# First feed-forward's weights loaded a second time, two bytes off, so that one mask gives the low half's 25 bits

## Chip, cores and metric

One core of one Trainium2 chip. The metric is device microseconds for one execution of the whole program, the median of three runs.

## What is computed

Eight images of 576 tokens go through a packed attention (32 packed queries, 8 heads of 64), then through two feed-forwards. The first is the one that the change touches:

```python
h = x @ w_in                                   # x 4608x512, w_in 512x2048
g = h * (1.0 / (1.0 + np.exp(-1.702 * h)))
x = (g @ w_out).astype(np.float32)             # w_out 2048x512
h = np.maximum(np.maximum(x @ w1, x @ w2), x @ w3)
out = (h @ w_out2).astype(np.float32)
```

`w_in` and `w_out` arrive as float64, eight bytes a number. The kernel sees each number as two 32-bit words, low word first.

## The kernel before

**Numbers in two parts.** TensorE multiplies fp32r operands. To keep float32 accuracy every operand is held as a high and a low part, and `mm3` (lines 102 to 104) makes a product of three matmuls: low by high, high by low, high by high.

**Conversion of a weight.** `load_raw` (L136) brings one raw tile of 128 x 2048 words on the SP queue as two DMAs of 512 KB. `convert` (L142) makes from it, on 1024 numbers per partition, the high part (rounded down to what fp32r holds) and the low part (the bits of the double that come below). In the text a step of it goes by its line:

- L148, DVE: the high word without sign and without its lowest 9 bits, into `tmp`; L149, ACT: its exponent put on float32's scale.
- L151, DVE: the lowest 9 bits of the high word, into the second half of `tmp`.
- L152, DVE: the 16 bits under them, read as a uint16 view of the low word, times 2^-16, added to L151's result. So the low part has 25 bits, built from two places of the raw double.
- L154, DVE: sign and L149's result joined; L157, ACT: the high part written to the weight tile.
- L158, DVE: sign and exponent alone, written back over the high word; L159, DVE: L152's 25 bits times 2^-20 times that power of two, the low part of the weight tile.

So a conversion has six DVE instructions and two ACT instructions, each over 128 x 1024. There are sixteen: for each quarter `n` of the hidden width two of `w_in` (`wi0_n`, `wi1_n`) and two of `w_out` (`wo4n`, `wo4n+2`).

**Tiles.** Raw tiles, `tmp`, finished weights and `pw` (the attention's packed values multiplied into `w_in`, one tile for each image and quarter) share one pool, `w_tile`, of 16 buffers of 8 KB per partition. The eight `wo` tiles stay for the whole feed-forward. A new tile waits for the last reader of the one that had its buffer.

**Stages.** Attention of images 0 and 1 comes first, the conversions run beside it and beside the first units of the feed-forward. A unit `n` is one (image, half of the tokens, 128 hidden columns): `h_unit` makes `h` on TensorE, takes tanh on ACT (L495) and joins it on DVE (`t`, L496); `g_unit` splits the result (ACT L501, DVE L503); `out_unit`, two units later, adds it to four `acc` banks. At the end of four or eight units DVE and ACT move `acc` out (L523, L527, L529). The units of images 0 and 1 go by quarters of the hidden width, so each quarter of the weights is first read at a certain unit: quarter 1 at unit 16, quarter 2 at unit 32, quarter 3 at unit 36. Images 0 and 1 take 64 units, and from the 64th on nothing is converted for this feed-forward. The second feed-forward ends the program.

**What sets the order.** Every step is put in a list with a time of its own (`add`), the list is sorted and traced, and the tile framework's scheduler then orders each engine's instructions and places the tiles. At run time each engine, and the SP queue, goes through its instructions strictly in that order.

Of the kernel before, what the change touches and what calls it, by code (L numbers as in the profile page):

```python
# [10 lines left out]
I32 = mybir.dt.int32  # L11
U16 = mybir.dt.uint16
AF = mybir.ActivationFunctionType
ALU = mybir.AluOpType
# [6 lines left out]
TB = 512  # L21
# [12 lines left out]
L_ = [8.18, 16.49, 4, 22.39]  # L34
Z_ = [1, 1, 1, 0, 0, 0, 0, 0, 0, 0, 0, 0, 0, 0, 0, 0]
# [7 lines left out]
def tile_packed_attention_moe(  # L43
# [13 lines left out]
    nc = tc.nc  # L57
# [19 lines left out]
    def f(t):  # L77
        return t.bitcast(F32)

    def i(t):  # L80
        return t.bitcast(I32)


    def w_tile(name, dt=F32R):
        return wp.tile([P, 2, 2, TB], dt, tag="w", name=name)
# [29 lines left out]
    rebias = const.tile([P, 1], F32, name="rebias")  # L115
# [20 lines left out]
    def load_raw(name, srcs):  # L136
        raw = w_tile(f"raw_{name}", I32)
        for x, src in enumerate(srcs):
            nc.sync.dma_start(raw[:, x].rearrange("p a b -> p (a b)"), src)
        return raw  # L140

    def convert(name, raw, pool):  # L142
        h = raw.rearrange("p x a (b w) -> p (x a b) w", w=2)[:, :, 1]
        m = raw.bitcast(U16).rearrange("p x a (b w) -> p (x a b) w", w=4)[:, :, 1]
        tmp = w_tile(f"tmp_{name}", I32)
        t1, t2 = (tmp[:, x].rearrange("p a b -> p (a b)") for x in range(2))
        w = w_tile(name)
        nc.vector.tensor_scalar(out=t1, in0=h, scalar1=0x7FFFFE00, scalar2=None, op0=ALU.bitwise_and)  # L148
        nc.scalar.activation(t1, t1, AF.Relu, scale=8.0, bias=rebias)  # L149
        yield  # L150
        nc.vector.tensor_scalar(out=t2, in0=h, scalar1=0x1FF, scalar2=None, op0=ALU.bitwise_and)  # L151
        nc.vector.scalar_tensor_tensor(out=f(t2), in0=m, scalar=2.0 ** -16, in1=t2, op0=ALU.mult, op1=ALU.add)  # L152
        yield
        nc.vector.scalar_tensor_tensor(  # L154
            out=t1, in0=h, scalar=-2 ** 31, in1=t1, op0=ALU.bitwise_and, op1=ALU.bitwise_or
        )
        nc.scalar.copy(w[:, :, 0], f(tmp[:, 0]))  # L157
        nc.vector.tensor_scalar(out=h, in0=t1, scalar1=-2 ** 23, scalar2=None, op0=ALU.bitwise_and)  # L158
        nc.vector.scalar_tensor_tensor(  # L159
            out=w[:, :, 1], in0=f(tmp[:, 1]), scalar=2.0 ** -20,  # L160
            in1=f(raw).rearrange("p x a (b w) -> p x (a b) w", w=2)[:, :, :, 1], op0=ALU.mult, op1=ALU.mult
        )
        yield w
# [246 lines left out]
    wi = {}  # L410
# [39 lines left out]
    wo = {}  # L450
# [94 lines left out]
    def c_tile(name):  # L545
        if "f" in late:
            return late["r"].tile([P, TB], F32R, tag="c", name=name)
        return u_tile(name, F32R)[:, :TB]

    def conv_late(name, raw, hi, lo, n):  # L550
        t1, t2 = (late["r"].tile([P, TB], I32, tag="c", name=f"c{y}_{name}") for y in range(2))
        h = raw.rearrange("p (a w) -> p a w", w=2)[:, :, 1]
        m = raw.bitcast(U16).rearrange("p (a w) -> p a w", w=4)[:, :, 1]
        nc.vector.tensor_scalar(out=t1, in0=h, scalar1=0x7FFFFE00, scalar2=None, op0=ALU.bitwise_and)
        nc.scalar.activation(t1, t1, AF.Relu, scale=8.0, bias=rebias)
        nc.vector.tensor_scalar(out=t2, in0=h, scalar1=0x1FF, scalar2=None, op0=ALU.bitwise_and)
        nc.vector.scalar_tensor_tensor(out=f(t2), in0=m, scalar=2.0 ** -16, in1=t2, op0=ALU.mult, op1=ALU.add)
        nc.vector.scalar_tensor_tensor(
            out=t1, in0=h, scalar=-2 ** 31, in1=t1, op0=ALU.bitwise_and, op1=ALU.bitwise_or
        )  # L560
        nc.scalar.copy(hi, f(t1))
        nc.vector.tensor_scalar(out=h, in0=t1, scalar1=-2 ** 23, scalar2=None, op0=ALU.bitwise_and)
        nc.vector.scalar_tensor_tensor(
            out=lo, in0=f(t2), scalar=2.0 ** -20, in1=f(raw).rearrange("p (a w) -> p a w", w=2)[:, :, 1],
            op0=ALU.mult, op1=ALU.mult
        )
        return f(t1), f(t2)


    class Piece:  # L570
# [11 lines left out]
        def conv(self):  # L582
            self.hl = [c_tile(f"wa{y}_{self.n}") for y in range(2)]
            self.v, self.s = conv_late(self.n, self.raw, *self.hl, TB)
# [213 lines left out]
    def add(t, fn, *a):  # L798
        plan.append((t, len(plan), fn, a))

    def conv(t, name, src, store, load=6.0, pool=0, step=0.0):
        raws, it = [], []

        def a():
            raws.append(load_raw(name, src))

        def b_():
            it.append(convert(name, raws[0], pool))
            next(it[0])

        def c_():
            next(it[0])

        def d_():
            store(next(it[0]))

        add(t - load, a)
        add(t, b_)
        add(t + step, c_)
        add(t + 2 * step, d_)  # L820
# [13 lines left out]
    def main():  # L834
# [10 lines left out]
        t = T0  # L845
# [13 lines left out]
        def wi_save(g, n):  # L859
            nc.gpsimd.dma_start(f(wsc[g, n].rearrange("c p a b -> p c a b")), f(sv[g, n]))  # L860

        def wi_store(g, n):
            def s(ws):
                sv[g, n] = ws
                if W_[n] == 0:
                    wi_save(g, n)
                for c in range(2):
                    wi[0, 2 * g + c, n] = ws[:, c]
            return s

        def wo_store(fc):
            def s(ws):
                wo[fc], wo[fc + 1] = (ws[:, x] for x in range(2))
            return s

        kk = 0
        for n in range(NQ):
            def tc_(kk):
                base = 7 + 6.49 * kk if n == 0 else tn[start[0, n]] - 22 + 7 * (kk - 4 * n)
                return base + K_[kk]  # L880
            for g in range(2):
                t = tc_(kk)
                conv(t, f"wi{g}_{n}", [w_in[2 * g, n], w_in[2 * g + 1, n]], wi_store(g, n), L_[kk] if kk < 4 else 19, Z_[kk], 0.0)
                if W_[n] > 0:
                    add(t + W_[n], wi_save, g, n)
                kk += 1
                for b in range(2):
                    add(max(t + .1, tn[start[b, n]] - PL_[b], tpt[b, g]), pw1_unit, b, g, n)
            for fc in range(4 * n, 4 * n + 4, 2):
                conv(tc_(kk), f"wo{fc}", [w_out[fc], w_out[fc + 1]], wo_store(fc), L_[kk] if kk < 4 else 19, Z_[kk], 0.0)  # L890
                kk += 1


# [35 lines left out]
        for idx in range(18):  # L929
            pc = Piece(idx // 2, idx % 2)  # L930
            t = TP + idx * TP_[1] if idx < 14 else TB0 - 10 + (idx - 14) * 10.5
# [5 lines left out]
        for fc in range(NF2):  # L937
            t = max(TP + 14 * TP_[1] + TP_[2] * fc, tn[225])
# [39 lines left out]
    if True:  # L978
        main()
        for _, _, fn, a in sorted(plan, key=lambda s: s[:2]):  # L980
            fn(*a)
        late["f"].release()
        late["x"].release()
        spp.release()
# [53 lines left out]
```

## Time and profile before

| | |
|---|---|
| median of 3 runs | 1418.73 us (1418.44 to 1420.18) |
| the profiled execution's own time | 1418.77 us |
| its span, first to last instruction | 1416.9 us |
| busy: TensorE (PE) | 1344.9 us, 95% of the span |
| busy: VectorE (DVE) | 989.1 us, 70% |
| busy: ScalarE (ACT) | 575.2 us, 41% |
| busy: GpSimd (POOL) | 322.6 us, 23% |
| read from HBM / written | 191.89 MB / 43.78 MB |

Busy time is the union of an engine's instructions. A matmul's end is modelled, so PE's share says where PE was held up rather than how near it is to its peak. [...]

### The profile page before, as it was taken

The page shows a single profiled execution, that of the slowest core. Times are in us where ns is not written, and L with a number is a line of the kernel's source. Part 1 is how long each engine was busy: PE and PEld are TensorE (multiplying, and loading weights), DVE is VectorE, ACT ScalarE, POOL GpSimd, SP SyncE. Part 2 cuts the span into 40 slices and gives each one's busy share as a digit, 9 for nine tenths or more (in the row PEclk, how much of TensorE's full clock was granted, in tenths as well). Part 3 has the DMA queues.
Part 4 walks back from the last instruction along what each step waited for, and adds up shares of the span by engine and source line. Part 5 has one row for each costly group of instructions (what it writes and reads, how often), then busy time and mean ns, then how long its engine had stood idle before and what let it go on. Part 6 is the DMA issues. An engine that isn't in the chain of part 4 may idle for free.

```text
span 1416.9 us, 22472 instructions
## 1 busy us (share of the span) xinstructions
PE 1344.9 (95%) x8450; PEld 1278.2 (90%) x8450; DVE 989.1 (70%) x1850; ACT 575.2 (41%) x1212; POOL 322.6 (23%) x436
## 2 busy tenths in 40 slices
PE   5899789999999999999999899699999999999998
PEld 3688789999999989999888899699989999899997
DVE  6799897887666566759899977564646646466362
ACT  3555555664554555545555552131221311213111
POOL 1110244344331035314344222101101001011000
PEclk8999899999999999999999999899999999999999
DMA  8654313561442224125655539765747747476461
GB/s 310 240 189 150 113 55 108 160 198 42 124 127 77 94 66 131 58 75 190 201 173 173 172 126 299 256 227 174 258 161 248 269 160 250 169 259 216 144 205 45
DMA packets 88524, 237.13 MB, mean 167 GB/s; under 512 B 10848, under 2 KB 40032, under 8 KB 81504
## 3 DMA queue, kind: packets, MB, share of 16 engines
q0 software_dynamic: 24640, 132.66, 27.8%
q1 hardware_dynamic: 63776, 103.05, 21.9%
q8 instruction: 66, 1.08, 0.3%
q14 instruction: 42, 0.34, 0.1%
HBM read 191.89 MB, written 43.78 MB: 166 GB/s over the span
## 4 chain that ended last, share of the span: by engine, by line
PE 75%; DVE 16%; DMA 3%; issue 2%; ACT 2%; POOL 1%; SPq 1%; DVEq 0%; ACTq 0%; POOLq 0%
PE p L102 9%; PE p L103 8%; PE p L104 8%; PE acc L102 7%; PE acc L103 7%; PE acc L104 7%; PE accb L103 3%; PE accb L104 3%; PE accb L102 3%; PE h L102 3%; PE h L104 3%; PE h L103 3%; DVE g L503 2%; DVE t L496 2%; DMA xr<-x2d 1%
## 5 line engine op out<-in xcount | busy, mean ns | idle before, releaser
L102 PE MATMUL acc<-g,wo 128*128 128x288 f32 x1024 | 306.3, 302 | 16.2 <-DVE x L523 5.9
L103 PE MATMUL acc<-g,wo 128*128 128x288 f32 x1024 | 303.8, 297 | 7.6 <-DVE g L503 7.5
L104 PE MATMUL acc<-g,wo 128*128 128x288 f32 x1024 | 303.7, 297 | 0.0
L102 PEld LDWEIGHTS acc<-g,wo 128*128 128x128 f32 x1024 | 194.4, 191 | 22.6 <-issue 6.3
L103 PEld LDWEIGHTS acc<-g,wo 128*128 128x128 f32 x1024 | 195.2, 191 | 12.6 <-DVE g L503 10.2
L104 PEld LDWEIGHTS acc<-g,wo 128*128 128x128 f32 x1024 | 195.2, 191 | 0.7 <-issue 0.3
L503 DVE TENSOR_TENSOR g<-t,g 128x288 fp32r<-128x288 f32 x254 | 142.6, 562 | 44.4 <-ACT g L501 41.2
L501 ACT CAST g<-t 128x288 fp32r<-128x288 f32 x256 | 110.8, 433 | 150.9 <-DVE t L496 149.7
L102 PE MATMUL h<-at,pw 128*128 128x288 f32 x512 | 154.8, 303 | 6.0 <-DVE t L496 4.1
L495 ACT ACTIVATE t<-h 128x288 f32<-128x288 f32 x256 | 104.4, 409 | 123.4 <-PE h L104 120.4
L496 DVE SCALAR_TENSOR_TENSOR t<-t,h 128x288 f32<-128x288 f32 x256 | 114.8, 450 | 55.1 <-ACT t L495 52.6
L103 PE MATMUL h<-at,pw 128*128 128x288 f32 x512 | 152.7, 298 | 0.3 <-POOL at L127 0.3
L104 PE MATMUL h<-at,pw 128*128 128x288 f32 x512 | 152.2, 297 | 0.0
L628 POOL DMA_DIRECT2D wa<-wsa x54 | 28.7, 532 | 426.2 <-PE p L104 413.2
L102 PE MATMUL p<-x_T,ws 128*128 128x384 f32 x324 | 109.3, 337 | 11.4 <-DVE m L717 11.4
L103 PE MATMUL p<-x_T,ws 128*128 128x384 f32 x324 | 109.0, 336 | 0.0
L104 PE MATMUL p<-x_T,ws 128*128 128x384 f32 x324 | 108.8, 336 | 0.0
L717 DVE TENSOR_TENSOR u<-s,p 128x384 f32<-128x384 f32 x54 | 29.9, 554 | 112.7 <-PE p L104 112.7
L102 PEld LDWEIGHTS h<-at,pw 128*128 128x128 f32 x512 | 97.0, 190 | 9.6 <-DVE t L496 6.5
L103 PEld LDWEIGHTS h<-at,pw 128*128 128x128 f32 x512 | 97.1, 190 | 0.7 <-POOL at L127 0.5
L104 PEld LDWEIGHTS h<-at,pw 128*128 128x128 f32 x512 | 97.2, 190 | 0.2
L747 ACT COPY s<-p 128x384 f32<-128x384 f32 x54 | 25.9, 479 | 163.3 <-PE p L104 163.3
(187 smaller groups left out, 3150.6 us busy)
## 6 DMA issues: line engine op xcount, KB each, us to landing
ws<-wss POOLq DMA_DIRECT2D x54, 1024.0 KB, 7.6
wa<-wsa POOLq DMA_DIRECT2D x54, 768.0 KB, 4.6
wi<-wsc POOLq DMA_DIRECT2D x48, 512.0 KB, 4.0
raw_k<-in_k SPq DMA_DIRECT2D x32, 288.0 KB, 3.3
raw_q<-in_q SPq DMA_DIRECT2D x32, 288.0 KB, 2.8
x2d<-x SPq DMA_DIRECT2D x16, 576.0 KB, 3.5
wraw<-in_w SPq DMA_DIRECT2D x72, 128.0 KB, 3.3
wss<-ws SPq DMA_DIRECT2D x36, 256.0 KB, 3.0
```

The costliest lines, as they stand in the source:

```text
L102: nc.tensor.matmul(o, al, bh, start=start, stop=False, skip_group_check=more)
L103: nc.tensor.matmul(o, ah, bl, start=False, stop=False, skip_group_check=more)
L104: nc.tensor.matmul(o, ah, bh, start=False, stop=stop, skip_group_check=more)
L495: nc.scalar.activation(t, o, AF.Tanh, scale=0.5 * 1.702)
L496: nc.vector.scalar_tensor_tensor(out=t, in0=t, scalar=1.0, in1=o, op0=ALU.add, op1=ALU.mult)
L501: latest["act"] = nc.scalar.copy(g[:, 0], gt[n])
L503: latest["dve"] = eng.tensor_tensor(out=g[:, 1], in0=gt[n], in1=f(g[:, 0]), op=ALU.subtract)
L628: nc.gpsimd.dma_start(a, wsa[n % 9].rearrange("p i h b f -> p (i h b f)"))
L717: latest["dve"] = nc.vector.tensor_tensor(out=o, in0=a, in1=b, op=op)
L747: latest["act"] = nc.scalar.copy(self.s1, self.b1)
```

## The change

From the fifth conversion on (twelve of sixteen: all of quarters 1 to 3) a second tile, `low`, is loaded 10 units of the list's time ahead of the conversion. It holds the same float64 numbers, but its source starts two bytes later, so every 32-bit word of `low` straddles the border of the two words of a double: its lowest 25 bits are the 9 and the 16 bits that L151 and L152 put together before. One mask then gives them as an integer, and the last instruction reads that integer with another power of two. `tmp` is gone: its first half now lies in the raw tile's low words (which nothing reads any more), its second half in `low`. All operands but the finished weight are therefore every other 32-bit word of a tile.

```diff
+    def load_low(name, srcs):
+        low = w_tile(f"low_{name}", I32)
+        for x, src in enumerate(srcs):
+            to = low[:, x].rearrange("p a b -> p (a b)").bitcast(U16)
+            nc.sync.dma_start(to[:, :4 * TB - 1], src.bitcast(U16)[:, 1:])
+        return low
+
+    def convert_low(name, raw, low):
+        h, t1 = (raw.rearrange("p x a (b w) -> p (x a b) w", w=2)[:, :, y] for y in (1, 0))
+        t2 = low.rearrange("p x a (b w) -> p (x a b) w", w=2)[:, :, 0]
+        fr, lr = (f(t).rearrange("p x a (b w) -> p x (a b) w", w=2) for t in (raw, low))
+        w = w_tile(name)
+        nc.vector.tensor_scalar(out=t1, in0=h, scalar1=0x7FFFFE00, scalar2=None, op0=ALU.bitwise_and)
+        nc.scalar.activation(t1, t1, AF.Relu, scale=8.0, bias=rebias)
+        yield
+        nc.vector.tensor_scalar(out=t2, in0=t2, scalar1=0x1FFFFFF, scalar2=None, op0=ALU.bitwise_and)
+        yield
+        nc.vector.scalar_tensor_tensor(
+            out=t1, in0=h, scalar=-2 ** 31, in1=t1, op0=ALU.bitwise_and, op1=ALU.bitwise_or
+        )
+        nc.scalar.copy(w[:, :, 0], fr[:, :, :, 0])
+        nc.vector.tensor_scalar(out=h, in0=t1, scalar1=-2 ** 23, scalar2=None, op0=ALU.bitwise_and)
+        nc.vector.scalar_tensor_tensor(
+            out=w[:, :, 1], in0=i(lr)[:, :, :, 0], scalar=2.0 ** -36, in1=fr[:, :, :, 1], op0=ALU.mult, op1=ALU.mult
+        )
+        yield w
...
-    def conv(t, name, src, store, load=6.0, pool=0, step=0.0):
+    def conv(t, name, src, store, load=6.0, pool=0, step=0.0, low=0.0):
...
+        def a2():
+            raws.append(load_low(name, src))
+
+        if low:
+            add(t - low, a2)
...
-            it.append(convert(name, raws[0], pool))
+            it.append(convert_low(name, *raws) if low else convert(name, raws[0], pool))
...
-                conv(t, f"wi{g}_{n}", [w_in[2 * g, n], w_in[2 * g + 1, n]], wi_store(g, n), L_[kk] if kk < 4 else 19, Z_[kk], 0.0)
+                conv(t, f"wi{g}_{n}", [w_in[2 * g, n], w_in[2 * g + 1, n]], wi_store(g, n), L_[kk] if kk < 4 else 19, Z_[kk], 0.0, 0 if kk < 4 else 10)
...
-                conv(tc_(kk), f"wo{fc}", [w_out[fc], w_out[fc + 1]], wo_store(fc), L_[kk] if kk < 4 else 19, Z_[kk], 0.0)
+                conv(tc_(kk), f"wo{fc}", [w_out[fc], w_out[fc + 1]], wo_store(fc), L_[kk] if kk < 4 else 19, Z_[kk], 0.0, 0 if kk < 4 else 10)
```

In the changed kernel the steps have the lines L155 (was L148), L158 (the mask, in the place of L151 and L152), L160 (was L154), L164 (was L158) and L165 (was L159) on DVE, L156 and L163 on ACT; `t` is L524, `g` L531, `acc` moves out at L551, and the second load is L147.

The scheduler orders both programs anew, so instructions move against each other as well. DVE around unit 20, before the change (`t_20` opens unit 20 on DVE; `pw_1_1` is image 1's packed product for quarter 1; `x2_3` collects an image's result):

```order
L131 TENSOR_TENSOR pw_1_1_1131<-pw_1_0_1_1132,pw_1_1_1131 128x512
L159 SCALAR_TENSOR_TENSOR wi0_2_1119<-tmp_wi0_2_1118,raw_wi0_2_861 128x2x512
L131 TENSOR_TENSOR pw_1_1_1131<-pw_1_1_1_1141,pw_1_1_1131 128x512
L503 TENSOR_TENSOR g_19_1162<-t_19_1115,g_19_1162 128x288
L496 SCALAR_TENSOR_TENSOR t_20_1172<-t_20_1172,h_20_1165 128x288
L148 TENSOR_SCALAR tmp_wi1_2_1190<-raw_wi1_2_918 128x1024
L503 TENSOR_TENSOR g_20_1187<-t_20_1172,g_20_1187 128x288
L151 TENSOR_SCALAR tmp_wi1_2_1190<-raw_wi1_2_918 128x1024
L496 SCALAR_TENSOR_TENSOR t_21_1207<-t_21_1207,h_21_1200 128x288
L152 SCALAR_TENSOR_TENSOR tmp_wi1_2_1190<-raw_wi1_2_918,tmp_wi1_2_1190 128x1024
```

At `t_20` five of the twelve conversions are done (`wi1_1`, `wi0_1`, `wo4`, `wo6`, `wi0_2`), and `wi1_2` begins behind it. The same place of DVE after the change:

```order
L158 TENSOR_SCALAR low_wi1_2_1033<-low_wi1_2_1033 128x1024
L524 SCALAR_TENSOR_TENSOR t_19_1125<-t_19_1125,h_19_1118 128x288
L165 SCALAR_TENSOR_TENSOR wo6_1081<-low_wo6_958,raw_wo6_834 128x2x512
L165 SCALAR_TENSOR_TENSOR wi0_2_1128<-low_wi0_2_990,raw_wi0_2_863 128x2x512
L531 TENSOR_TENSOR g_19_1170<-t_19_1125,g_19_1170 128x288
L155 TENSOR_SCALAR raw_wi1_3_1075<-raw_wi1_3_1075 128x1024
L165 SCALAR_TENSOR_TENSOR wi1_2_1198<-low_wi1_2_1033,raw_wi1_2_923 128x2x512
L131 TENSOR_TENSOR pw_1_1_1139<-pw_1_0_1_1140,pw_1_1_1139 128x512
L131 TENSOR_TENSOR pw_1_1_1139<-pw_1_1_1_1149,pw_1_1_1139 128x512
L524 SCALAR_TENSOR_TENSOR t_20_1180<-t_20_1180,h_20_1173 128x288
```

Here six conversions are done at `t_20`, and the first step of a seventh (`wi1_3`).

The SP queue from the load of `wo4` on, before the change (`q_2_0_1`, `praw_3_0` and `k_3_0_0` are attention inputs of images 2 and 3):

```order
L139 DMA raw_wo4_800<-in_w_out 128x1024 x2
L139 DMA raw_wo6_832<-in_w_out 128x1024 x2
L139 DMA raw_wi0_2_861<-in_w_in 128x1024 x2
L139 DMA raw_wi1_2_918<-in_w_in 128x1024 x2
L210 DMA raw_q_2_0_1_1644<-in_q 128x576
L177 DMA praw_3_0_1767<-in_p 128x64
L210 DMA raw_k_3_0_0_1769<-in_k 128x576
L139 DMA raw_wi1_3_1063<-in_w_in 128x1024 x2
```

Four raw tiles go out ahead of `q_2_0_1`. After the change:

```order
L147 DMA low_wi1_1_593<-in_w_in 128x2047 x2
L147 DMA low_wi0_1_606<-in_w_in 128x2047 x2
L139 DMA raw_wo4_802<-in_w_out 128x1024 x2
L139 DMA raw_wo6_834<-in_w_out 128x1024 x2
L139 DMA raw_wi0_2_863<-in_w_in 128x1024 x2
L238 DMA raw_q_2_0_1_1657<-in_q 128x576
L238 DMA raw_k_3_0_0_1783<-in_k 128x576
L147 DMA low_wo4_910<-in_w_out 128x2047 x2
L139 DMA raw_wi1_2_923<-in_w_in 128x1024 x2
L147 DMA low_wo6_958<-in_w_out 128x2047 x2
L147 DMA low_wi0_2_990<-in_w_in 128x2047 x2
L147 DMA low_wi1_2_1033<-in_w_in 128x2047 x2
```

Now `q_2_0_1` and `k_3_0_0` stand ahead of `low_wo4` and of the four tiles behind it, and `praw_3_0` has moved far back.

## Rows read from the trace of the kernel before

**Rows 1.** The page: the span.

```profile
span 1416.9 us, 22472 instructions
```

**Rows 2.** Busy by stretches: PE, PEld, DVE, ACT, POOL, then PEclk, DMA share, GB/s.

```profile
60.00:100.00 40.00, 38.05 (x235) 34.16 (x234) 34.56 (x66) 22.28 (x48) 8.30 (x7) 0.96 0.56 201
100.00:120.00 20.00, 20.00 (x144) 19.39 (x143) 18.98 (x33) 12.22 (x24) 0.00 (x0) 1.00 0.41 152
120.00:160.00 40.00, 33.75 (x223) 31.46 (x222) 38.92 (x65) 19.65 (x34) 2.88 (x4) 0.96 0.40 155
160.00:200.00 40.00, 34.88 (x214) 32.82 (x215) 36.74 (x66) 22.84 (x47) 15.53 (x14) 0.87 0.25 78
200.00:217.00 17.00, 13.97 (x103) 13.23 (x103) 15.02 (x29) 7.95 (x17) 8.11 (x11) 1.00 0.28 90
217.00:1417.00 1200.00, 1165.22 (x7403) 1120.65 (x7401) 803.21 (x1520) 466.18 (x998) 279.15 (x380) 0.99 0.50 166
```

**Rows 3.** Waits of PE, 60 to 217 us: in total, times, longest.

```profile
PE acc L102 <- DVE x L523: 5.9, 3, 3.6
PE acc L103 <- DVE g L503: 4.9, 2, 2.6
PE h L102 <- DVE t L496: 2.3, 3, 1.4
PE ptp L335 <- DVE pn L328: 1.2, 2, 0.8
```

**Rows 4.** The chain of waits, 60 to 217 us: shares by line, then two pieces.

```profile
by line: PE acc L103 8.8%; PE acc L102 8.6%; PE acc L104 8.6%; PE h L102 4.0%; DVE g L503 4.0%; PE h L104 3.9%; PE h L103 3.9%; issue 3.5%; DVE tmp_wo L154 3.3%; DVE t L496 3.2%; DVE tmp_wi L152 3.0%; DVE tmp_wo L152 2.9%; DVE tmp_wo L151 2
...
85.39 2.34 DVE tmp_wi L152
...
179.87 1.77 DVE tmp_wo L152
```

**Rows 5.** The timeline of DVE: start, length, instruction.

```profile
101.05 0.68 DVE L148 TENSOR_SCALAR tmp_wo<-raw_wo 128x1024 int32<-128x1024 int32 x1
101.65 0.69 DVE L151 TENSOR_SCALAR tmp_wo<-raw_wo 128x1024 int32<-128x1024 int32 x1
102.37 1.22 DVE L152 SCALAR_TENSOR_TENSOR tmp_wo<-raw_wo,tmp_wo 128x1024 f32<-128x1024 uint16 x1
103.51 0.45 DVE L496 SCALAR_TENSOR_TENSOR t<-t,h 128x288 f32<-128x288 f32 x1
...
125.60 0.46 DVE L496 SCALAR_TENSOR_TENSOR t<-t,h 128x288 f32<-128x288 f32 x1
```

**Rows 6.** The costliest groups of DVE by shape, 60 to 217 us.

```profile
L154 DVE SCALAR_TENSOR_TENSOR tmp_wi<-raw_wi,tmp_wi 128x1024 int32<-128x1024 int32 x6 | 7.3, 1223 | 0.0
...
L131 DVE TENSOR_TENSOR pw<-pw,pw 128x512 fp32r<-128x512 f32 x10 | 6.8, 688 | 3.6 <-ACT pw L130 3.6
```

**Rows 7.** Line 158, 60 to 217 us: shortest, median, longest in ns.

```profile
L158 DVE TENSOR_SCALAR raw_wi<-tmp_wi x6: 655/692/1546, 75.9 to 153.6; 128x1024 int32<-128x1024 int32 x6
```

**Rows 8.** The page's DMA issues: count, KB each, us to landing.

```profile
raw_wi<-in_w_in SPq DMA_DIRECT2D x16, 512.0 KB, 6.5
raw_wo<-in_w_out SPq DMA_DIRECT2D x16, 512.0 KB, 7.0
```

**Rows 9.** Busy by stretches, 40 to 50 us, columns as in rows 2.

```profile
40.00:50.00 10.00, 8.99 (x41) 6.79 (x41) 8.56 (x16) 6.71 (x14) 1.40 (x1) 1.00 0.93 340
```

**Rows 10.** SP's timeline and its longest wait, 60 to 100 us.

```profile
97.28 0.67 SPq L210 DMA_DIRECT2D raw_k<-in_k  x1
98.00 0.91 SPq L139 DMA_DIRECT2D raw_wi<-in_w_in  x2
...
SPq L210 <- POOL k L127: 19.5, 1, 19.5
```

## The prediction

> **What bounds the kernel now.** The page first: a span of 1416.9 us [rows 1], and a profiled execution of 1418.77 us, so 1.9 us lie around the span. The sum below is made against 1418.8 us; the median of the runs, 1418.73, is the same number for this purpose. A measurement of this kernel tells a change from none at about 0.2%, 2.8 us.
>
> The second view is busy time by stretches [rows 2]. The reader is to see three kinds of stretch there. From 217 us on PE is busy 1165 of 1200 us, DVE 803: the long steady part belongs to TensorE and no weight of the changed kind is converted in it, so the change can only give or take time before. From 100 to 120 us PE is busy all 20 us, and DVE 19: both are full, and a lighter DVE alone wins nothing. From 120 to 200 us DVE is busy 38.9 and 36.7 of 40, while PE is busy 33.8 and 34.9: there DVE is the engine that is full and PE is the one that waits. PE's idle time is 2.0 us from 60 to 100 us, and 6.2 + 5.1 + 3.0 = 14.4 us from 120 to 217 us. Its granted clock is a mean of 0.96, then 0.87, in the two stretches in which it keeps waiting, 1.00 before and after: the busy 33.8 and 34.9 us hold 1.4 + 4.5 = 5.9 us that full clock would not have needed. So 20.3 us could be won behind 120 us at the very most.
>
> The third view, PE's waits, says who ends them [rows 3]: DVE, with 14.3 us in the four largest, through its ordinary steps (the move of `acc`, the split `g`, the join `t`); none of the four is a step of a conversion. That is what a full in-order queue looks like: the short instruction that PE needs stands behind a long one. The fourth, the chain of waits, shows the long ones [rows 4]: L152 alone has 3.0% and 2.9% of the 157 us from 60 to 217, which is 9.3 us.
>
> **The change, part by part.** *Removed: L152.* The start of one instruction to the start of the next counts, since the ends overlap: 0.60 us for a mask (101.05 to 101.65), 1.14 us for a two-source instruction such as L152 (102.37 to 103.51) [rows 5]. A conversion has three of each, 5.22 us of DVE; afterwards three and two, 4.08. Twelve conversions give 12 x 1.14 = 13.7 us less on DVE.
>
> *Where that falls* is told by the order. `t_20` starts at 125.60 us [rows 5]. Ahead of it stood five conversions, 26.1 us; afterwards six and a mask, 25.1 us: 1.0 us less, in a stretch where PE is full anyway. Behind it stood seven, 36.5 us; afterwards six less a mask, 23.9 us. So 12.7 of the 13.7 us leave DVE exactly where it is full and PE waits. The new order does the reading of L155, L160 and L164 well ahead of the unit that needs the weight, which puts no PE work behind it that was not there.
>
> *How much of 12.7 us reaches the end.* The upper bound is all of it, since PE's own loss behind 120 us, 20.3, is larger. The lower one is what L152 holds of the chain there: 9.3 less the one early piece of 2.34 us is 6.9, and of the piece of 1.77 us the part above 1.14 stays (0.6: I assume that what lengthened it meets the next instruction instead) [rows 4]: 6.3. I take the middle, 9.5, because the chain moves to the next cause when one is taken out, while clock comes back when PE's pauses shorten. With half of the 1.0 us from ahead of `t_20` that is 10.0 us.
>
> *Moved: operands at every second word.* L158, the old one, writes every second word at a median of 0.692 us [rows 7], as fast as the masks that only read so, 0.68 and 0.69 [rows 5]. L154 has one source at every second word: 1223 ns for 1024 columns against 688 for L131's 512 with nothing skipped [rows 6], 1.04 ns for each further column, so the skipping is free there. I price the new forms as the old. No row has three such operands in one two-source instruction (L160) or two such sources (L165); that is a rival below. ACT's two steps change in the same way and have cover: ACT is busy 20 to 23 of 40 us from 120 to 200 us [rows 2].
>
> *Added: 24 DMAs, 12.6 MB.* On SP each costs about 0.45 us to issue (0.91 for a pair) [rows 10], 11 us in all, on a queue that spends its time waiting. At the 340 GB/s of the busiest stretch [rows 9] they need 37 us of all DMA engines, spread over 130 us in which the DMA share is 0.25 to 0.56 [rows 2]. I take nothing for them; at half that rate they would need 74 us and just fit, on average.
>
> *Moved on SP:* the two loads of `low` for quarter 1 go out ahead of `wo4` and delay it by 2 us; `wo4`'s first step starts at 101.05 us [rows 5], and its tile was asked for ahead of the wait of 19.5 us that ends before 97.28 [rows 10], so nothing of it is seen. What matters is `q_2_0_1` and `k_3_0_0`: they wait for POOL to split two other tiles, up to 19.5 us, and `k_3_0_0` went out at 97.28, the next raw tile at 98.00 [rows 10]. Now five tiles stand behind that wait, four of them `low`. If the wait ends as before, they go from 98 us on; a tile lands some 7 us after its issue [rows 8] and the next ones 3.1 us apart (1.05 MB at 340 GB/s): at 105, 108, 111, 114 and 117 us. DVE's need: `t_13` starts at 103.51 and `t_20` at 125.60, 3.2 us a unit. `low_wo4` is read behind `g_13`, about 105; `low_wo6` behind `t_16`, 113; `low_wi0_2` behind `g_17`, 117; `low_wi1_2` behind `g_18`, 120. The first is just in time, the others have 2 or 3 us. I take nothing, with up to 5 us kept for the range. Later loads of `low` wait for a buffer that a finished conversion or `pw` gives back, as the raw tiles do now; with each some 10 us or more until it is read.
>
> **Sum:** 1418.8 - 10.0 = **1408.8 us**. From the terms' bounds alone: 1418.8 - 12.7 - 1.0, and up to 2 us more if PE's clock stays up, is 1403; 1418.8 - 6.3 + 5 is 1417.5.
>
> **The rivals.** *The new waits eat the gain.* If the `low` tiles move at half the rate (their source starts two bytes into a row, and no row has such a transfer), the five land 6.2 us apart, the last at 130 instead of 117 us, 10 us behind its need; DVE is in order, so `t_19` and everything behind stand still. That costs about what the change wins: 1418 to 1420 us. For it: the first tile has no margin at all. Against: each row of a tile is one run of 4,094 bytes, and PE has work in hand for some units. It decides from a landing about 4 us later than I reckon.
>
> *Slower: every second word costs after all.* The masks do 1024 columns in 0.60 us, a two-source instruction in 1.14, so the masks run at twice its rate. If reading and writing every second word of the same tile took that away, 36 masks would each lose 0.54 us: 19.4 - 13.7 = 5.8 us more on the full DVE, 1424.6 us. It decides from 13.7 / 36 = 0.38 us a mask. Against it: rows 5 and 7 have each half of that at full speed. [...]
>
> *A small gain.* The relief comes, but PE then meets its own work, or the attention's POOL and ACT steps, at once: only half of the lower bound, 3 to 4 us, 1415 us. For it: POOL is busy 15.5 of 40 us from 160 to 200 us and splits the attention's inputs there [rows 2]. Against: POOL is among none of PE's large waits [rows 3].
>
> That the low half would not hold the same 25 bits changes no instruction's length, so it is no rival for the time.
>
> **How the numbers follow.** The forecast gets 0.68, the small gain 0.15, the new waits 0.10 (0.07 of it within 0.2%, 0.03 beyond), every second word 0.07, of which I put 0.01 within 0.2% (a smaller loss that only cancels the gain). Faster by over 0.2% is 0.68 + 0.15 = 0.83; within 0.2% 0.08; slower by over 0.2% 0.03 + 0.06 = 0.09. The range of 8 in 10 runs from 1402.5 us, where the whole relief arrives and the clock stays up, to 1416 us, which takes in the small gain and leaves out the cases at and above no change.
>
> **What would show it.** Right: DVE has 12 instructions less and about 13.7 us less busy time; L160 and L165 take 1.22 us and L155, L158 and L164 0.69; PE's idle time between 120 and 217 us falls from 14.4 us to 5 or so and its granted clock there rises to 0.95 or more; the steady part keeps its length; the last conversion's L165 ends some 8 to 12 us earlier than its L159 did. Wrong: DVE idle with a DMA of `low` as the releaser, most likely around 105 us; L160 or L165 well above 1.22 us; PE's waits moved to ACT or POOL with the same sum; a second feed-forward or a steady part that grew by what the first 217 us lost.

## The result, and the profile after

The changed kernel takes **1402.26 us** (median; 1401.52 to 1404.8) against 1419.45 us for the kernel before on the same chip: a ratio of 0.988, 95% interval 0.9862 to 0.9898. Timed once more with other experiments it had 1402.24 us, ratio 0.9891 (0.9874 to 0.9907). The direction was forecast; the gain is 17 us where the prediction had 10, and the time lies 0.24 us below the range. Ratios compare executions in the fast state alone; one execution of e13_first5 below (4626 us) was in the slow one and is left out. The profiled execution of the changed kernel took 1404.8 us, 14.0 less than the one before (1418.77), so the traces hold 14 of the 17 us.

The page after: span, then busy time of each engine. DVE has twelve instructions less and 15.0 us less busy time (989.1 before), 13.7 of it by the prediction's own count.

```profile
span 1402.7 us, 22504 instructions
...
PE 1340.6 (96%) x8450; PEld 1274.0 (91%) x8450; DVE 974.1 (69%) x1838; ACT 576.9 (41%) x1212; POOL 322.1 (23%) x436
```

Where in the span: SP's timeline has the first store of a finished image's result to `x2d`, an event that both programs have at the same point of the work. Before:

```profile
214.60 0.60 SPq L535 DMA_DIRECT2D x2d<-x  x1
```

After:

```profile
201.70 0.60 SPq L563 DMA_DIRECT2D x2d<-x  x1
```

It comes 12.9 us earlier (14.4 in the profile of the second timing). From there to the end are 1202.3 us before (1416.9 - 214.6) and 1201.0 after (1200.1 in the second): the steady part kept its length within 2 us, and the gain lies ahead of it. Up to 60 us PE is busy for the same time in both, 39.0 and 39.6 us. So the stretch to read is the one from 60 us to that store. In busy time by stretches (columns as in rows 2), before:

```profile
60.00:214.60 154.60, 138.24 (x895) 128.66 (x894) 142.31 (x250) 83.37 (x165) 34.25 (x34) 0.94 0.39 139
```

After, first the same row, then the stretches that answer to [rows 2]:

```profile
60.00:201.70 141.70, 133.42 (x906) 125.78 (x906) 128.22 (x241) 84.21 (x166) 35.80 (x36) 0.99 0.65 241
...
60.00:100.00 40.00, 38.62 (x244) 34.88 (x244) 36.50 (x67) 23.05 (x48) 10.06 (x9) 1.00 0.58 218
100.00:120.00 20.00, 19.53 (x137) 18.54 (x136) 18.45 (x38) 11.62 (x25) 0.00 (x0) 1.00 0.94 378
120.00:160.00 40.00, 38.07 (x275) 36.95 (x275) 38.06 (x69) 27.39 (x48) 7.75 (x7) 1.00 0.93 340
160.00:200.00 40.00, 35.51 (x242) 33.70 (x241) 33.51 (x66) 21.30 (x45) 18.00 (x20) 0.96 0.31 101
200.00:217.00 17.00, 17.00 (x123) 16.46 (x122) 13.33 (x31) 9.72 (x23) 6.31 (x6) 1.00 0.40 123
```

The reader is to split the 12.9 us in two. PE's **idle** time falls from 154.60 - 138.24 = 16.4 us to 8.3: 8.1 us. Its **busy** time falls from 138.2 to 133.4: 4.8 us, and the row has a cause for it: the mean granted clock (PEclk, TensorE's clock as a share of full speed) was 0.94 and is 0.99. These traces show it at two levels: of the 309 half-microsecond slices from 60 to 214.5 us before, 273 have 1.00, 28 have 0.50, and eight lie between. At 0.50 the matmuls of 128x288 into `h` start 0.24 us apart (170.82, 171.06, 171.31 us), at 1.00 0.13 us apart (154.27, 154.40, 154.53). By these slices the mean of 0.94 is some 17 us at the lower level, and 0.99 some 3 us. In the prediction's own stretches, from 120 to 217 us, idle time is 1.9 + 4.5 + 0 = 6.4 us (14.4 before), and of the busy time the lower clock takes 0.04 x 35.5 = 1.4 us (5.9 before).

At 60 us the two programs are not at quite the same point (895 and 906 matmuls follow up to the store). From the start it is 1031 in both. Before:

```profile
0.00:214.60 214.60, 177.23 (x1031) 155.14 (x1032) 184.00 (x327) 107.39 (x211) 42.89 (x56) 0.93 0.49 176
```

After:

```profile
0.00:201.70 201.70, 173.00 (x1031) 151.59 (x1032) 169.36 (x315) 108.70 (x211) 42.87 (x56) 0.99 0.68 249
```

So PE's idle time falls by 8.7 us and its busy time by 4.2. The same rows read on DVE's side: 14.6 us less busy time (184.0 to 169.4), and idle time of 30.6 and 32.3 us. What left DVE arrived at the store, all but 1.7 us. These are two views of the same 12.9 us: PE's idle time and clock say where they show, and are not to be added to DVE's time.

Who ends the waits that are left, 60 to 205 us (in total, times, longest); [rows 3] had 14.3 us in four lines:

```profile
PE s L102 <- DVE a L399: 2.9, 1, 2.9
PE h L102 <- DVE t L524: 1.3, 2, 0.9
PE acc L103 <- DVE g L531: 1.3, 1, 1.3
PE pv L102 <- DVE pw L131: 1.0, 1, 1.0
```

The long waits on `x` and `g` are gone (0.5 and 1.3 us are left of 5.9 and 4.9); the largest is a step of the attention.

### The profile page after: what moved, and what is told of

The parts are those of the page before. It is cut to its first block, busy times and chain, and to the rows that moved or that the text cites. A ratio compares the mean times of both kernels' runs of the same rounds, so it can differ in the third digit from the quotient of the medians.

```text
span 1402.7 us, 22504 instructions
## 1 busy us (share of the span) xinstructions
PE 1340.6 (96%) x8450; PEld 1274.0 (91%) x8450; DVE 974.1 (69%) x1838; ACT 576.9 (41%) x1212; POOL 322.1 (23%) x436
## 4 chain that ended last, share of the span: by engine, by line
PE 73%; DVE 16%; DMA 5%; issue 2%; ACT 2%; POOL 1%; SPq 1%; DVEq 0%; ACTq 0%; POOLq 0%
PE p L102 9%; PE p L103 9%; PE p L104 9%; PE acc L102 6%; PE acc L103 6%; PE acc L104 6%; PE accb L104 3%; PE accb L103 3%; PE accb L102 3%; PE h L102 3%; PE h L104 3%; PE h L103 3%; DVE g L531 2%; DVE t L524 2%; DVE pw L131 1%
## 5 line engine op out<-in xcount | busy, mean ns | idle before, releaser
L531 DVE TENSOR_TENSOR g<-t,g 128x288 fp32r<-128x288 f32 x254 | 144.6, 569 | 46.3 <-ACT g L529 43.1
L524 DVE SCALAR_TENSOR_TENSOR t<-t,h 128x288 f32<-128x288 f32 x256 | 114.9, 449 | 53.7 <-ACT t L523 50.8
```

Source lines behind the costliest of these rows:

```text
L524: nc.vector.scalar_tensor_tensor(out=t, in0=t, scalar=1.0, in1=o, op0=ALU.add, op1=ALU.mult)
L531: latest["dve"] = eng.tensor_tensor(out=g[:, 1], in0=gt[n], in1=f(g[:, 0]), op=ALU.subtract)
```

## The experiments

Each kernel was timed in turn with the kernel before; ratios have a 95% interval. "DVE" is what the edit takes from or adds to DVE against the kernel before, at 1.14 us for each two-source instruction and 0.60 for a mask.

| kernel | DVE, us | second load | median, us | ratio to before |
|---|---|---|---|---|
| e12_twice | +13.7 | no | 1437.65 | 1.0135 (1.0116 to 1.0154) |
| before | 0 | no | 1418.4 to 1419.5 | 1 |
| e13_first5 | -5.7 | no | 1414.99 | 0.9973 (0.9964 to 0.9983) |
| e14_last7 | -8.0 | no | 1409.03 | 0.9934 (0.9919 to 0.9948) |
| e4_nojoin | -13.7 | no | 1403.9 | 0.9886 (0.9871 to 0.9901) |
| e1_twosrc12 | 0 | yes | 1414.14 | 0.996 (0.9949 to 0.9972) |
| e3_twosrc_last6 | -6.8 | yes | 1407.69 | 0.9915 (0.9899 to 0.993) |
| e2_twosrc_first6 | -6.8 | yes | 1405.64 | 0.9901 (0.9886 to 0.9916) |
| changed kernel | -13.7 | yes | 1402.26 | 0.988 (0.9862 to 0.9898) |
| e8_no_exp | -20.9 | yes | 1403.37 | 0.9883 (0.9865 to 0.99) |
| e5_tmp | -13.7 | yes, and `tmp` | 1419.35 | 1.0002 (0.9988 to 1.0015) |
| e16_tmp_lead3 | -13.7 | yes, and `tmp` | 1415.42 | 0.9976 (0.9966 to 0.9986) |

Theory 1 was that DVE's time is the whole gain; theory 2, that half or more comes from the second tile and the order it brings; theory 3, that the second loads cost something which the relief hides.

**e1_twosrc12: the old DVE work in the new program.** Behind each L158:

```diff
+        nc.vector.scalar_tensor_tensor(
+            out=t2, in0=t2, scalar=0x1FFFFFF, in1=t2, op0=ALU.bitwise_and, op1=ALU.bitwise_and
+        )
```

> The changed kernel, with a two-source instruction of 128 x 1024 put back behind every mask L158 (twelve, about 1.14 us each on DVE, so DVE has its old 13.7 us again, while the second loads, their buffers and the absence of tmp stay). Theory 1, the relief of DVE is the whole gain: 1416 to 1421 us, PE idle 120 to 217 us back at 12 us or more. Theory 2, half or more of the gain comes from the second tile and the order that goes with it (the scheduler begins conversions earlier): 1404 to 1411 us. Theory 3, the second loads themselves cost something that the relief hides: above 1421 us.

1414.14 us, between the ranges of theories 1 and 2: 11.9 above the changed kernel, 5.4 below the kernel before. PE is idle for 10.6 us from 120 to 217 us, where theory 1 asked for 12 or more. Theory 1 has the larger part, and theory 2 a smaller one. Theory 3 falls as it was put.

**e4_nojoin: relief alone, in the old program.** `short` is set for the twelve conversions.

```diff
-        nc.vector.scalar_tensor_tensor(out=f(t2), in0=m, scalar=2.0 ** -16, in1=t2, op0=ALU.mult, op1=ALU.add)
+        if not short:
+            nc.vector.scalar_tensor_tensor(out=f(t2), in0=m, scalar=2.0 ** -16, in1=t2, op0=ALU.mult, op1=ALU.add)
...
-            out=w[:, :, 1], in0=f(tmp[:, 1]), scalar=2.0 ** -20,
+            out=w[:, :, 1], in0=tmp[:, 1] if short else f(tmp[:, 1]), scalar=2.0 ** -20,
```

> The kernel before with L152 left out in the same twelve conversions and nothing else changed: no second load, tmp as it was; the 16 lower bits of those weights' low part are left out. DVE has 13.7 us less. Theory 1: as fast as the changed kernel, 1401 to 1406 us. Theory 2: 1408 to 1413 us. Theory 3, the second loads cost something: faster than the changed kernel, under 1400 us.

1403.9 us: 15.6 us won by 13.7 us of DVE, with no second load (the scheduler orders this program anew too). That is theory 1, and by the medians a little more than one for one. With the 5.4 us of e1_twosrc12 it would be 21 us, more than the 17 of the changed kernel: the two parts overlap. Its row from 60 us to the first store:

```profile
60.00:202.66 142.66, 132.47 (x905) 123.50 (x905) 131.84 (x242) 82.88 (x166) 35.39 (x36) 1.00 0.42 151
```

PE's idle time is 10.2 us (6.2 less than before), its busy time 5.8 us less, the clock a mean of 1.00. From the start:

```profile
0.00:202.66 202.66, 172.46 (x1032) 149.65 (x1033) 171.58 (x315) 106.39 (x211) 42.48 (x56) 1.00 0.52 186
```

DVE has 12.4 us less busy time than before and the same idle time (31.1 against 30.6 us), and the store comes 11.9 us earlier. So in this profile the relief arrives about one for one, with the clock in it. This execution (1406.43 us) was the slowest of its kernel; that the clock makes the medians' excess over one for one is argued and not shown.

**e12_twice: the same step in the other direction.** `two` is set for the twelve conversions.

```diff
+        if two:
+            nc.vector.scalar_tensor_tensor(out=f(t2), in0=f(t2), scalar=1.0, in1=f(t2), op0=ALU.mult, op1=ALU.max)
```

> The kernel before with one more two-source instruction behind L152 in the twelve conversions (a product by 1.0 and a maximum with itself, the value stays; about 13.7 us more on DVE, no second load). If every us of DVE in the stretch where it is full reaches the end, and TensorE's clock suffers as well: 1432 to 1436 us. If only the share that the chain of waits shows does (6.3 of 13.7): 1424 to 1427 us.

1437.65 us, above both ranges: 18.4 us lost by 13.7 us of DVE, 1.35 for one. The row to the first store, which comes at 235.0 us:

```profile
60.00:235.00 175.00, 145.78 (x906) 134.07 (x907) 159.80 (x267) 84.72 (x167) 37.66 (x36) 0.91 0.35 123
```

PE's idle time is 29.2 us, 12.9 more, and its busy time grows by 7.5 us at a clock of 0.91. From the start:

```profile
0.00:235.00 235.00, 184.65 (x1031) 159.58 (x1032) 198.89 (x339) 107.78 (x211) 44.71 (x56) 0.93 0.45 160
```

DVE is busy 14.9 us more and idle 5.5 us more (36.1 us): here something beyond its own time is lost. From 60 us to the store its waits for ACT's steps grow from 8.6 to 12.5 us. The chain's share (6.3 of 13.7) prices neither direction.

**e13_first5 and e14_last7: where the relief counts.** As e4_nojoin, with `4 <= kk < 9` and `kk >= 9` for the conversions concerned.

> The kernel before without L152 in the five conversions that stand ahead of unit 20 on DVE (wi1_1, wi0_1, wo4, wo6, wi0_2; 5.7 us of DVE less; the 16 lower bits of their low parts are left out). By the prediction's step (work ahead of unit 20 lies where TensorE is full and brings at most a part): 1417 to 1419.5 us. If the queue of DVE is one backlog that begins before unit 20, so that work taken out early lets everything behind it start earlier: 1412 to 1415 us.

> The kernel before without L152 in the seven conversions behind unit 20 (wi1_2 to wo14; 8.0 us of DVE less; the 16 lower bits of their low parts are left out). By the prediction's step, all of the gain that the leaving out in twelve brought, 1403 to 1407 us. If the backlog begins earlier: 1409 to 1412 us, and this and the run with the first five add up.

4.2 us for 5.7 us of DVE (3.8 by the ratio), and 10.2 us for 8.0. Behind unit 20 a microsecond of DVE is worth 1.27; ahead of it some 0.7, neither nothing nor all. The two add up to 14.4 of e4_nojoin's 15.6. Both times lie in the ranges for a backlog that begins ahead of unit 20, the first at the very edge, and outside those of the prediction's step.

**e2 and e3: half of the old work in the new program.** The edit of e1_twosrc12 under `if two:`, with `kk < 10` and `kk >= 10`.

> The same two-source instruction behind the mask of the first six changed conversions alone (those of quarter 1, wi0_2 and wi1_2; 6.8 us more on DVE, nearly all ahead of unit 20, where PE was full and DVE nearly so). Theory 1 in its narrow form, only DVE work behind unit 20 reaches the end: 1402 to 1405 us. Theory 1 in its wide form, work ahead of unit 20 is pushed back in DVE's queue and arrives as well: 1408 to 1411 us. Theory 2: under 1404 us.

> The same instruction behind the mask of the last six changed conversions (wi1_3 to wo14; 6.8 us more on DVE behind unit 19, where it is full). Theory 1: 6.8 us and some clock, 1409 to 1412 us. Theory 2: under 1405 us.

3.4 and 5.4 us for 6.8 us of DVE each, against 1402.26 us; both times fall between their ranges. Both together (e1_twosrc12) cost 11.9. That the first microseconds are cheaper is likely, but 3 us is little beside intervals of some 2 us for each time: the changed kernel would then be near the point where DVE no longer decides.

**e8_no_exp: 7.2 us of relief beyond.** L164 left out.

```diff
-        nc.vector.tensor_scalar(out=h, in0=t1, scalar1=-2 ** 23, scalar2=None, op0=ALU.bitwise_and)
```

> The changed kernel without L164 in the twelve conversions (0.60 us each, 7.2 us in all; the low half is then multiplied by the whole high word and not by its power of two). If DVE's time still arrives in full at the end: 1394 to 1397 us. If TensorE is now close to its floor there (its idle time of 6.4 us from 120 to 217 us, of which ACT and POOL end a part): 1398 to 1401 us.

1403.37 us (1399.41 to 1403.49), above both ranges: no faster in the median. The row to its first store, at 199.85 us, shows 7.2 us of idle time where the changed kernel has 8.3:

```profile
60.00:199.85 139.85, 132.64 (x902) 124.75 (x902) 123.14 (x228) 83.88 (x165) 35.73 (x36) 0.99 0.66 244
```

So a microsecond of DVE is worth 1.35 us where L152 was doubled, 1.1 in the kernel before (0.7 ahead of unit 20, 1.27 behind it), 0.5 to 0.9 where it was put back into the changed kernel, and next to nothing beyond the changed kernel. What sets this floor is open: 7.2 us of PE's idle time remain, and DVE waits for landings of `low` for 2.8 us from 120 to 205 us.

**e5_tmp and e16_tmp_lead3: the second load without the room for it.** Both masks write into a `tmp` tile again; e16 also loads `low` 3 units ahead in place of 10.

```diff
+        tl = low.rearrange("p x a (b w) -> p (x a b) w", w=2)[:, :, 0]
+        tmp = w_tile(f"tmp_{name}", I32)
+        t1, t2 = (tmp[:, x].rearrange("p a b -> p (a b)") for x in range(2))
...
-        nc.vector.tensor_scalar(out=t2, in0=t2, scalar1=0x1FFFFFF, scalar2=None, op0=ALU.bitwise_and)
+        nc.vector.tensor_scalar(out=t2, in0=tl, scalar1=0x1FFFFFF, scalar2=None, op0=ALU.bitwise_and)
...
```

> The changed kernel with tmp back as a tile of its own (both masks write into it), so a conversion holds four of the sixteen buffers and its first step needs a new one; the DVE instructions are those of the changed kernel, 13.7 us less than before. If only the DVE time counts: 1401 to 1405 us. If the buffers count (the first steps work in place and so can stand early in DVE's order; here they stand behind unit 4 for the first conversion and behind unit 18 for wo4, later than in the kernel before): 1410 us or more, with DVE idle ahead of unit 18 and full behind it.

> e5_tmp with the second load 3 units of the list's time ahead of the conversion in place of 10, so the second tile holds its buffer for a shorter time; the first step of wo4 stands behind unit 14 on DVE (in e5_tmp behind 18, in the kernel before behind 12), that of wo6 behind 19 (21; 16). Same DVE instructions as the changed kernel. If the place of the conversions is what e5_tmp lost: between e5_tmp and the changed kernel, 1408 to 1414 us. If the second load as such is dear beside tmp: still 1417 us or more.

1419.35 us, as the buffers' range had it, and 1415.42, between its two ranges. The DVE instructions of the changed kernel, and none or a quarter of its gain. The stretches of e5_tmp:

```profile
60.00:100.00 40.00, 36.26 (x231) 32.32 (x230) 33.07 (x63) 22.00 (x47) 9.14 (x7) 1.00 0.87 325
100.00:120.00 20.00, 20.00 (x142) 19.32 (x140) 11.94 (x25) 9.42 (x21) 0.00 (x0) 1.00 0.34 126
120.00:160.00 40.00, 32.27 (x226) 30.34 (x225) 36.60 (x61) 21.77 (x37) 2.51 (x3) 1.00 0.78 280
```

DVE is idle for 15.0 us from 60 to 120 us (6.5 before), busy 36.6 of the next 40, and there PE misses 7.7 of 40 us. The relief was spent as idle time early, because the conversions stand late in the order. Which unit's `t` they follow on DVE, from the order of the programs (first step to last step; -1 is ahead of unit 0):

```
conversion   before   changed   e1       e4       e5_tmp   e16
wi1_1        3-6      -1-4      -1-7     3-4      4-7      4-7
wo4          12-14    7-16      7-16     12-14    18-19    14-16
wi1_2        20-21    14-19     16-21    19-21    22-22    21-21
wi1_3        23-25    19-24     23-25    23-25    26-28    24-25
```

In the changed kernel the first steps stand 4 to 6 units earlier than before; in e1 the first three do by 4 or 5, and `wi1_3` stands where it stood. They work in place, in tiles that a load has filled, and need no new buffer; with `tmp` they need one from a pool that now also holds `low`. The traces bear it out: behind 120 us DVE still has 33.3 us of conversion in the changed kernel and 40.2 in e4, whose first stores come at 201.7 and 202.7 us, but 45.5 in e5_tmp, 46.9 in e16, 47.3 in e1 and 49.4 before, whose first stores come at 211.4 to 214.6 us. That the early place is what e1 gains (5.4 us) stays argued, from this and from e16, which moves places and time together; no run moved the places alone.

**The lead of the second load.** The changed kernel with 5, 12 and 16 units in place of 10:

```diff
-L_[kk] if kk < 4 else 19, Z_[kk], 0.0, 0 if kk < 4 else 10)
+L_[kk] if kk < 4 else 19, Z_[kk], 0.0, 0 if kk < 4 else 5)
```

> The changed kernel with the second load 5 units ahead in place of 10; nearly the same order on DVE. If a tile's landing decides (each lands some 8 us after its issue and DVE already waited 3.6 us in all): more idle time of DVE on low and 1404 to 1409 us. If the wait for a buffer decides when a load can go, and not its place in the list: 1401 to 1404 us.

> The changed kernel with the second load 12 units ahead; nearly the same order on DVE. 1401 to 1404 us if the landings have margin, 1399 to 1401 us if DVE's 3.6 us of waiting for low was a cost that an earlier load takes away.

> The changed kernel with the second load 16 units ahead: the buffers run short at the other end, wo12 and wo14 are begun behind units 28 and 32 and ended behind 41 (in the changed kernel 33 and 36). If only DVE's time counts: 1401 to 1404 us. If the place counts: 1406 us or more, with TensorE waiting between 170 and 200 us.

1401.72, 1402.16 and 1402.45 us (ratios 0.9878, 0.9889, 0.9879): no difference. My expectation for 16 units, that two conversions ended late would cost 4 us, was wrong.

**e7_aligned: the two bytes.**

```diff
-            nc.sync.dma_start(to[:, :4 * TB - 1], src.bitcast(U16)[:, 1:])
+            nc.sync.dma_start(to, src.bitcast(U16))
```

> The changed kernel with the second load from the row's own start, 4,096 bytes a row in place of 4,094 two bytes on; same order on every engine. The low halves' 25 bits are then taken from other bits of the numbers. If the offset of two bytes costs nothing: 1401 to 1404 us and the same landing times of low (7.9 us in the middle). If it costs: landings nearer to the 6.5 to 7.0 us of raw tiles, DVE's idle time on low (3.6 us) gone, 1397 to 1400 us.

1403.79 us (ratio 0.9899, 0.9883 to 0.9916), the same within what the runs tell. From issue to landing (least, middle, most), the changed kernel, and then e7_aligned:

```profile
DMA to landing us min/median/max: 3.7/7.9/17.7
```

```profile
DMA to landing us min/median/max: 3.6/8.1/18.6
```

Rows of 4,094 bytes that start two bytes on landed in 7.9 us in the middle, those of 4,096 in 8.1.

**e9_wo2: the same trick in the second feed-forward's weights**, 764 to 800 us, as an attempt at a faster kernel.

```diff
+        if fc % 2 == 0:
+            late["low"] = w_tile(f"low_o{fc}", I32)
+        low = late["low"][:, fc % 2].rearrange("p a b -> p (a b)")
+        nc.sync.dma_start(low.bitcast(U16)[:, :4 * TB - 1], w_out2[fc].bitcast(U16)[:, 1:])
```

(and the steps of `convert_low` over 128 x 512 in `conv_wo2`).

> The changed kernel with the same trick in the six conversions of the second feed-forward's output weights (128 x 512 each, 764 to 800 us): second load into a w tile, both steps in place, the two-source instruction of 0.60 us gone, 3.6 us of DVE less. In the changed kernel DVE is busy 40.0 of 40 us from 760 to 800 us and PE 33.1. If relief arrives in full wherever DVE is full and PE waits: 1398 to 1400 us. If the waits there are due to something else (POOL's and ACT's part in the same stretch): 1401 to 1404 us.

1407.56 us, above both ranges and slower than the changed kernel by some 5 us. From 740 to 830 us DVE's waits have a new line:

```profile
DVE low_o L658 <- DMA low_o<-in_w_out: 3.6, 2, 2.7
```

The wait for the tile that makes the step possible is as long as what the step saves, 3.6 us of DVE. That would account for no gain; where the further loss arises was not settled. No kernel here is clearly faster than the changed one.

## Why the prediction was right and wrong

**What bounds the kernel: right.** DVE full, PE waiting, 120 to 200 us; the gain lies there, and the rest kept its length.

**The price of L152: right.** 13.7 us by starts; 15.0 of busy time went.

**"How much of 12.7 us reaches the end": the step that failed.** It took "the middle, 9.5" between all of it and 6.3, L152's place in the chain of waits, and so forecast 10.0 us where 17 came. The lower bound was none, and the middle was far too little: without L152 in the old program 15.6 us came of 13.7 (e4_nojoin), with it twice 18.4 were lost (e12_twice). The chain names one instruction of the queue; in the traces DVE's idle time up to the first store stays at 30.6 to 32.3 us (before, e4_nojoin, changed), so what is taken from its busy time arrives nearly whole, whichever instruction the chain names.

The clock was undersized too: it stood in the upper bound with "up to 2 us", and PE's busy time up to the store is 4.2 us less in the changed kernel and 4.8 less in e4_nojoin. It is a part of what DVE's relief brings and not a gain on top of it. In three of the profiles a higher clock goes with less idle time: 0.91, 0.94 and 0.99 at 29.2, 16.4 and 8.3 us (e12_twice, before, changed). These three agree with the prediction's "clock comes back when PE's pauses shorten", which was its author's assumption. But the amount of idle time alone does not set the mean: e5_tmp has 0.97 at 17.5 us of idle time, e3_twosrc_last6 0.95 at 10.0 (both from 60 us to the first store). What does set it was not shown.

Of the 17 us, the two profiles of the changed kernel show 12.9 and 14.4 ahead of the store and 1.3 and 2.2 behind it. The latter is less than profiles differ by there: from the store to the end the others take 1197.5 to 1203.9 us.

The prediction held its own correction. Under what would show it, it asked for PE's idle time to fall from 14.4 to 5 us and the clock to reach 0.95; by its own rows that is 9.4 us of idle time and, with 5% in place of 5.9 us lost of the 69 busy ones, some 2.5 us of clock: 11.9 us, not 10.0, and still short of 17. A sum and the rows that are to prove it have to give the same number.

**"Where that falls": half right.** 12.7 us behind `t_20` did count most (1.27 for one), but what is removed ahead of it counts too, some 0.7 (e13_first5), though PE is full there from 100 to 120 us: what DVE finishes early it need not do later. The last L165 starts at 185.6 us where the last L159 did at 202.4, 16.8 us earlier; 8 to 12 were forecast.

**Operands at every second word: right on DVE.** The conversions' rows after (shortest, median, longest, ns):

```profile
L155 DVE TENSOR_SCALAR raw_wi<-raw_wi x6: 656/682/690, 55.4 to 140.2; 128x1024 int32<-128x1024 int32 x6
L158 DVE TENSOR_SCALAR low_wi<-low_wi x6: 632/684/695, 77.2 to 142.7; 128x1024 int32<-128x1024 int32 x6
L160 DVE SCALAR_TENSOR_TENSOR raw_wi<-raw_wi x6: 1218/1227/1397, 58.2 to 143.6; 128x1024 int32<-128x1024 int32 x6
L165 DVE SCALAR_TENSOR_TENSOR wi<-low_wi,raw_wi x6: 1184/1215/1218, 78.2 to 146.1; 128x1024 fp32r<-128x1024 int32 x6
L165 DVE SCALAR_TENSOR_TENSOR wo<-low_wo,raw_wo x6: 1209/1216/1218, 113.6 to 185.6; 128x1024 fp32r<-128x1024 int32 x6
```

The `wo` forms of L155 and L160 have longer medians:

```profile
L155 DVE TENSOR_SCALAR raw_wo<-raw_wo x6: 676/1038/1902, 87.8 to 173.8; 128x1024 int32<-128x1024 int32 x6
L160 DVE SCALAR_TENSOR_TENSOR raw_wo<-raw_wo x6: 1215/1490/2458, 92.8 to 178.7; 128x1024 int32<-128x1024 int32 x6
```

Their shortest are as short as those of `wi`, and the three long ones of L160 lie beside splits on POOL (the last section); before, L152 had such pieces too (up to 2342 ns).

L165 before took a median of 1224 and 1214 ns as L159; with two sources at every second word it takes 1215 and 1216, or 1.19 ns a column. Three operands at every second word (L160 of `wi`, 1227 ns) cost what one did (L154, 1223 in the mean). The masks that read and write so have medians of 682 to 691 ns (L155 of `wi`, L158, L164), where the rival decided from 0.38 us more a mask.

**24 DMAs at nothing: nearly right.** At 100 to 120 us they run with 378 GB/s, and `low_wo4` went out at 98.68 us, where the prediction had 98, and was read at 106.87 without a wait. DVE waited for `low` twice, 1.4 and 2.2 us, at other places (before 142.65 and 178.05 us). The second is not hidden: the longest wait that PE has left, 2.9 us for `a`, ends behind it. DVE's timeline, then PE's:

```profile
178.05 0.69 DVE L158 TENSOR_SCALAR low_wo<-low_wo 128x1024 int32<-128x1024 int32 x1 [2.24 <-DMA low_wo<-in_w_out]
```

```profile
180.42 0.37 PE L102 MATMUL s<-k,pbd 128*128 128x288 f32 x1 [2.92 <-DVE a L399]
```

With a lead of 16 units neither wait is there, others stand in their place (2.1 us for a `wo` from L165), and leads of 5 to 16 units give the same time: what the loads cost at the end is within the noise.

**Not priced at all: the buffers.** The change takes `tmp` out and puts `low` in its place. The prediction gave this no term beyond half of the 1.0 us ahead of `t_20`. It lets the conversions start early, which is, as argued above, what e1_twosrc12 gains (5.4 us); with `tmp` kept beside `low` the whole gain is gone (e5_tmp).

**The rivals.** Every second word and the small gain did not come, and new waits came only as the 3.6 us of DVE above. In e5_tmp, with one buffer more in use, the whole gain is eaten, though not by landings: DVE waits for no `low` there from 60 to 217 us.

## What to carry to other kernels

Where an in-order engine is full and the main engine waits behind it, price the removed time at about one for one (here 1.1 by the medians, 0.7 ahead of unit 20), and expect it to end: 7.2 us more of it were worth nothing. The main engine's idle and slow time is the ceiling of the gain (20.3 us here, of which 17 came) and is not added to it. A line's share of the chain of waits bounds neither side. Check the sum against the rows that are to prove it. And ask of a scratch tile what its absence lets start earlier: the same relief with one buffer more in use brought nothing.

## What the runs showed of the hardware

**ACT pays a little for every second word.** L156 and L163 did the work of L149 and L157 on such operands. Before:

```profile
L149 ACT ACTIVATE tmp_wi<-tmp_wi,rebias x8: 1140/1149/1157, 10.0 to 149.7; 128x1024 int32<-128x1024 int32 x8
L157 ACT CAST wi<-tmp_wi x8: 1047/1050/1057, 13.3 to 153.3; 128x1024 fp32r<-128x1024 f32 x8
```

After:

```profile
L156 ACT ACTIVATE raw_wi<-raw_wi,rebias x6: 1213/1248/1279, 56.1 to 140.9; 128x1024 int32<-128x1024 int32 x6
L163 ACT CAST wi<-raw_wi x6: 1127/1138/1164, 75.0 to 144.9; 128x1024 fp32r<-128x1024 f32 x6
```

0.10 and 0.09 us more for 1024 columns. DVE waited for L156 twice, 1.6 us in all, from 60 to 120 us.

**DVE beside POOL.** L160 took 1.22 us with no split on POOL beside it (178.66 us) and 2.46 beside one. After, DVE's timeline and then POOL's:

```profile
163.56 2.46 DVE L160 SCALAR_TENSOR_TENSOR raw_wo<-raw_wo 128x1024 int32<-128x1024 int32 x1
```

```profile
163.44 1.48 POOL L127 TENSOR_TENSOR q<-raw_q,q 128x576 fp32r<-128x576 f32 x1 [6.10 <-PE pw L104]
```

The instruction grew by 1.24 us, nearly the time it lay beside POOL's (163.56 to 164.92). A mask grew too: L158, 0.69 us in the median, took 1.79 at 153.24 us beside a split of `v`. Not every instruction beside a split did: L165 took 1.21 us at 168.10 beside a split of `q` on POOL, which took 2.49 (168.13).
